# Windowed attention feeding two expert layers on one core: score products over 128 rows in place of 64, queries kept per head parity, four exp buffers in place of six

## The chip, the cores and the metric

One Trainium2 chip, one core of it. The time is device microseconds (us) of one launch. The kernel before: 823.67 us, the median of 3 runs (823.54 to 824.04).

## The reference

What is computed, in three stages. The change lies in the first.

```python
# q, k, v: (2, 8, 768, 64); n_global = 8, n_local = 96; all float32
scores = q @ k^T / 8
rel = pos[:, None] - pos[None, :]
keep = (pos[None, :] < n_global) | ((rel >= 0) & (rel < n_local))
scores = where(keep, scores - slope[h] * dist, -1e9)     # dist: |rel|, or n_local for far globals
a = exp(scores - max); a /= sum(a) + 1e-9
x = (a @ v) as (1536, 512)                               # heads side by side
xn = x / rms(x) * rms_g
x = (silu(xn @ w_gate) * (xn @ w_val)) @ w_out           # 512 -> 1536 -> 512
gates = top2(x @ w_router + softplus(x @ w_noise) * noise)   # 8 experts, softmax over two
out = sum over the two experts of gate * (relu(x @ w1[e]) @ w2[e])
```

## The kernel before

The 1536 tokens (two batches of 768) make 12 tiles of 128 rows; tiles 0 to 5 are the first batch, 6 to 11 the second. Attention works tile by tile and, within a tile, by four *pairs* of heads, so there are 48 pair steps.

**Per tile** (`prep`, line 312): the tile's queries and keys, 128 tokens by 8 heads by 64, are transposed on TensorE in four blocks of two heads (line 334). Heads 2c and 2c+1 share column block c: the even head lies in partitions 0 to 63 and the odd one in 64 to 127. ScalarE takes the transposed block out of PSUM (line 335). Tiles 0 to 5 keep float32 (`F32T = NB`, line 133); tiles 6 to 11 split each operand into a rounded part (ScalarE) and the rest (VectorE, lines 339 and 341). GpSimd copies the previous tile's and the global keys beside the tile's own (line 344).

**Per pair** (`scores`, line 358): for each of its two heads a product of queries and 256 keys (128 in the first tile of a batch). The operands are sliced to the head's 64 partitions (`sl`, line 370), so TensorE contracts 64 rows. In tiles 0 to 5 it is one float32 product, which the trace shows as two matmuls; in tiles 6 to 11 it is three products (rounded by rounded, rest by rounded, rounded by rest). VectorE then adds the bias and takes the row's minimum (line 380), ScalarE takes the exponential into a tile named `p` (line 383, six buffers), and one step later `turn` (line 388) transposes the two `p` tiles on TensorE (line 396) for the product with the values (`values`, lines 443 and 447). The four pairs are (0,2), (1,3), (4,6), (5,7) (line 115): both heads of a pair have the same parity.

**The order.** Pair steps 0 to 11 (tiles 0 to 2) run before any of the expert layer's products; there `busy` (line 213) puts three products of a blank tile behind each group, 69 in all. From step 12 on the steps are taken one by one between the products of the first layer (`up`, line 617, and `down`, line 643). The statements give the dependences; a scheduler of the framework then sets each engine's order from its own estimate of durations, and assigns the buffers of a pool in that order. Each engine works its list strictly in order. `clear_out` (line 243) writes 3 MB of zeros to the output from a small tile `zero`, which takes one of the buffers of `p`.

After the attention the rest of the first layer follows (to about 500 us), then eight expert steps of the second (lines 878, 894, 900), whose rows are gathered by indirect transfers (line 842) and transposed (line 852).

Of the kernel before, what the change touches and what calls it, by code (L numbers as in the profile page):

```python
# [9 lines left out]
F32 = mybir.dt.float32  # L10
F32R = mybir.dt.float32r
# [94 lines left out]
def fused(ctx: ExitStack, tc: tile.TileContext, q, k, v, n_global, n_local, w_gate, w_val, w_out,  # L106
# [7 lines left out]
    NP = H // 2  # L114
    pair = [(4 * (p // 2) + p % 2, 4 * (p // 2) + p % 2 + 2) for p in range(NP)]
    DC = DM // P
# [11 lines left out]
    FEED = [1, 0, 0, 0, 1, 1, 3, 2, 2, 2, 3]  # L128
    START = 12
    LAG = 8  # L130
    NRAW = {"a": 12, "b": 7}
# [24 lines left out]
    def build_bias():  # L156
        rel = sb.tile([P, 2 * P], F32, name="rel", tag="n2", bufs=N2)
        msk = sb.tile([P, 2 * P], F32, name="msk", tag="s", bufs=4)
        tmp = at.tile([P, 2 * P], F32, name="tmp", tag="p", bufs=6)
        nc.gpsimd.iota(rel, pattern=[[-1, 2 * P]], base=P, channel_multiplier=1,  # L160
# [3 lines left out]
        nc.vector.tensor_mul(msk, msk, tmp)  # L164
        rel0 = at.tile([P, P], F32, name="rel0", tag="p", bufs=6)
        msk0 = at.tile([P, P], F32, name="msk0", tag="p", bufs=6)
        nc.vector.tensor_scalar(rel0, rel[:, P:], -float(n_local), None, op0=ALU.add)
# [36 lines left out]
    def small_loads():  # L204
# [4 lines left out]
        nc.sync.dma_start(nz, noise.rearrange("(t p) e -> p t e", p=P))  # L209
    blank = sb.tile([P, 512], BF16, name="blank")  # L210
    nc.gpsimd.memset(blank, 0.0)

    def busy(k, behind):

        pz = ps.tile([P, 512], F32, name=f"idle{behind.ins.name}", tag="v")
        for _ in range(k):
            follow(nc.tensor.matmul(pz, blank[:, :P], blank, start=True, stop=True).ins, behind.ins)

# [24 lines left out]
    def clear_out():  # L243
        zero = at.tile([P, P], F32, name="zero", tag="p", bufs=6)
        nc.gpsimd.memset(zero, 0.0)
        nc.sync.dma_start(out.rearrange("(p t) (c d) -> p (t c) d", p=P, d=P),
                            zero.rearrange("p (o d) -> p o d", o=1).broadcast_to([P, NT // P * DC, P]))
# [15 lines left out]
    def follow(a, b):  # L263
        tc.add_manual_dep(a, b.name, mybir.DependencyInfo(mybir.DependencyClass.NoSync, mybir.DependencyReason.DATA),
                          reason="order")

    xTh = {}
    xTl = {}
# [37 lines left out]
    def vsplit(ti, vn):  # L306
# [3 lines left out]
        return vn, rn  # L310

    def prep(ti, wide):
        b, i = divmod(ti, NB)
# [6 lines left out]
        if full:  # L320
            kT = [at.tile([P, NP, 2 * P], F32, name=f"kT{ti}", tag="kT0", bufs=2)] * 2
            qT = [at.tile([P, NP, P], F32, name=f"qT{ti}", tag="qT0", bufs=2)] * 2
        else:
            kT = [at.tile([P, NP, 2 * P], F32R, name=f"kT{ti}_{x}", tag=f"kT{x}", bufs=2) for x in range(2)]
            qT = [at.tile([P, NP, P], F32R, name=f"qT{ti}_{x}", tag=f"qT{x}", bufs=2) for x in range(2)]
        operands = ((kn, kT[0][:, :, P:], kT[1][:, :, P:], 1.0), (qn, qT[0], qT[1], -(D ** -0.5)))
        p3s = {}
        for cs, src, dh, dl, sc in ([(slice(0, NP),) + o for o in operands] if ti else
                                    [(slice(x, x + NP // 2),) + o for x in (0, NP // 2) for o in operands]):
            if sc not in p3s:  # L330
                p3s[sc] = bank("t", wide, f"pt{ti}").rearrange("p (a b) -> p a b", a=NP)
            p3 = p3s[sc]
            for c in range(cs.start, cs.stop):
                nc.tensor.transpose(p3[:, c, :], src.rearrange("p (a t) d -> p a (t d)", a=NP)[:, c, :], ident)
            nc.scalar.activation(dh[:, cs], p3[:, cs], AF.Copy, scale=sc)
            if full:
                continue
            if sc == 1.0:
                nc.vector.tensor_sub(dl, p3, dh.bitcast(F32))
            else:  # L340
                nc.vector.scalar_tensor_tensor(dl, p3, sc, dh.bitcast(F32), op0=ALU.mult, op1=ALU.subtract)

# [15 lines left out]
    def scores(u, wide):  # L358
# [9 lines left out]
        for t in range(2):  # L368
            h = pair[pr][t]
            sl = slice((h % 2) * D, (h % 2 + 1) * D)  # L370
            o = psc[:, t * W:(t + 1) * W]
            prods = ((0, 0), (1, 0), (0, 1)) if ti >= F32T else ((0, 0),)
            for n, (a, c) in enumerate(prods):
                mm = nc.tensor.matmul(o, qT[a][sl, h // 2, :], kT[c][sl, h // 2, C0:], start=(n == 0), stop=(n == len(prods) - 1))
        if wide:
            busy(3, mm)
        for t in range(2):
            h = pair[pr][t]
            s = sb.tile([P, 2 * P], F32, name=f"s{ti}_{h}", tag="s", bufs=4)
            nc.vector.tensor_tensor_reduce(s[:, :W], nb[:, h, :], psc[:, t * W:(t + 1) * W], 1.0, BIG * 10,  # L380
                                           op0=ALU.add, op1=ALU.min, accum_out=mx[:, h:h + 1])
            p = at.tile([P, 2 * P], F32, name=f"p{ti}_{h}", tag="p", bufs=6)
            nc.scalar.activation(p[:, :W], s[:, :W], AF.Exp, scale=-1.0, bias=mx[:, h:h + 1],  # L383
# [34 lines left out]
    def values(u, wide):  # L418
# [18 lines left out]
        for t in range(2):  # L437
            h = pair[pr][t]
            hs = slice(h * D, (h + 1) * D)
# [698 lines left out]
```

## Time and profile before

| | before |
|---|---|
| median of 3 runs | 823.67 us (823.54 to 824.04) |
| the profiled execution's span | 824.3 us |
| TensorE matmuls (PE) busy | 790.2 us (96%) |
| VectorE (DVE) busy | 456.8 us (55%) |
| ScalarE (ACT) busy | 358.3 us (43%) |
| GpSimd (POOL) busy | 298.7 us (36%) |
[...]
| line 374 (score products) | 240 matmul records, 47.5 us busy |

All times in the text are us from the start of the span unless ns is written. PE is the matmul side of TensorE, PEld its weight loads, which run beside it. Matmuls are pipelined: a row's duration runs from its start to its modelled end and overlaps its neighbours', so what a matmul costs the queue is the step from its start to the next start, not its duration. In a merged row (x6) the start is the first one's, and the duration runs to the last one's end.

### The profile page before, as it was taken

The page shows a single profiled execution, that of the slowest core. Times are in us where ns is not written, and L with a number is a line of the kernel's source. Part 1 is how long each engine was busy: PE and PEld are TensorE (multiplying, and loading weights), DVE is VectorE, ACT ScalarE, POOL GpSimd, SP SyncE. Part 2 cuts the span into 40 slices and gives each one's busy share as a digit, 9 for nine tenths or more (in the row PEclk, how much of TensorE's full clock was granted, in tenths as well). Part 3 has the DMA queues.
Part 4 walks back from the last instruction along what each step waited for, and adds up shares of the span by engine and source line. Part 5 has one row for each costly group of instructions (what it writes and reads, how often), then busy time and mean ns, then how long its engine had stood idle before and what let it go on. Part 6 is the DMA issues. An engine that isn't in the chain of part 4 may idle for free. (4 is left out here: it accounts for less than half of the span.)

```text
span 824.3 us, 13771 instructions
## 1 busy us (share of the span) xinstructions
PE 790.2 (96%) x5041; PEld 697.4 (85%) x5041; DVE 456.8 (55%) x1047; ACT 358.3 (43%) x798; POOL 298.7 (36%) x344
## 2 busy tenths in 40 slices
PE   8999999999999999999997997799999999999993
PEld 5778888988898888889896986788999999999982
DVE  4588845656478888334442566443444444445551
ACT  6766556555454343122331454343343334343430
POOL 5246521222276565001421135360434343434311
PEclk9999999999999999999998999899999999999997
DMA  8555421170233240010018003983373729272010
GB/s 185 129 141 143 130 48 27 39 192 15 78 104 121 83 128 0 1 52 23 12 20 229 26 27 107 335 255 109 106 211 121 234 94 277 75 248 73 33 40 34
DMA packets 116838, 88.76 MB, mean 108 GB/s; under 512 B 49449, under 2 KB 100649, under 8 KB 116768
## 3 DMA queue, kind: packets, MB, share of 16 engines
q1 hardware_dynamic: 107920, 65.43, 28.4%
q0 software_dynamic: 7120, 19.27, 7.0%
q10 hardware_dynamic: 1728, 3.15, 1.3%
q8 instruction: 41, 0.67, 0.4%
q14 instruction: 29, 0.24, 0.1%
HBM read 75.18 MB, written 13.34 MB: 107 GB/s over the span
## 5 line engine op out<-in xcount | busy, mean ns | idle before, releaser
L878 PE MATMUL pz<-gh,sa 128*128 128x256 f32 (+7 forms) x576 | 156.6, 339 | 0.8 <-issue 0.8
L878 PEld LDWEIGHTS pz<-gh,sa 128*128 128x128 f32 x576 | 103.3, 188 | 6.3 <-issue 1.0
L878 PE MATMUL pz<-gl,sa 128*128 128x256 f32 (+7 forms) x288 | 97.2, 338 | 0.9 <-issue 0.9
L643 PE MATMUL acc<-wo,dh 128*128 128x512 f32 x288 | 89.7, 403 | 0.1
L894 PE MATMUL ac<-zh,sb 128*128 128x480 f32 (+4 forms) x320 | 86.3, 364 | 0.0
L882 ACT ACTIVATE zh<-pz 128x256 fp32r<-128x256 f32 (+7 forms) x72 | 35.0, 487 | 110.2 <-PE pz L878 107.4
L883 DVE SCALAR_TENSOR_TENSOR zl<-pz,zh 128x256 fp32r<-128x256 f32 (+7 forms) x72 | 39.8, 552 | 75.6 <-ACT zh L882 65.3
L617 PE MATMUL pz<-xTh,wg 128*128 128x256 f32 x352 | 75.4, 289 | 0.3 <-DVE u L626 0.3
L617 PE MATMUL pz<-xTh,wv 128*128 128x256 f32 x352 | 75.1, 290 | 0.0
L599 ACT ACTIVATE sa<-wab 128x512 fp32r<-128x512 f32 x72 | 45.2, 630 | 57.0 <-PE ac L894 36.3
L617 PEld LDWEIGHTS pz<-xTh,wg 128*128 128x128 f32 x352 | 58.8, 191 | 4.6 <-issue 1.0
L630 POOL TENSOR_TENSOR dl<-u,dh 128x256 fp32r<-128x256 f32 (+1 forms) x38 | 36.9, 971 | 70.9 <-ACT dh L629 53.6
L603 DVE TENSOR_TENSOR sa<-wab,sa 128x512 fp32r<-128x512 f32 x51 | 36.7, 721 | 45.5 <-ACT sa L599 38.7
L894 PEld LDWEIGHTS ac<-zh,sb 128*128 128x128 f32 x320 | 57.9, 188 | 3.1
L617 PEld LDWEIGHTS pz<-xTh,wv 128*128 128x128 f32 x352 | 59.0, 193 | 0.5
L643 PEld LDWEIGHTS acc<-wo,dh 128*128 128x128 f32 x288 | 51.3, 190 | 9.3 <-issue 0.3
L878 PEld LDWEIGHTS pz<-gl,sa 128*128 128x128 f32 x288 | 54.3, 189 | 3.8 <-issue 1.1
L383 ACT ACTIVATE p<-s,mx 128x256 f32<-128x256 f32 (+1 forms) x96 | 46.3, 484 | 24.8 <-DVE mx L380 24.5
L783 POOL DMA_INDIRECT metad<-meta,si x24 | 24.5, 1023 | 84.2 <-DVE si L762 78.1
L842 POOL DMA_INDIRECT xg<-x2d,ic x30 | 30.0, 999 | 68.9 <-PE pg L852 62.4
L643 PE MATMUL acc<-wo,dl 128*128 128x512 f32 x144 | 54.1, 403 | 0.0
L894 PE MATMUL ac<-zl,sb 128*128 128x480 f32 (+4 forms) x160 | 53.0, 357 | 0.0
(251 smaller groups left out, 1831.7 us busy)
## 6 DMA issues: line engine op xcount, KB each, us to landing
wab<-in_moe_w_dram SPq DMA_DIRECT2D x128, 256.0 KB
rg<-in_moe_w_gate_dram SPq DMA_DIRECT2D x12, 512.0 KB
rv<-in_moe_w_val_dram SPq DMA_DIRECT2D x12, 512.0 KB
ro<-in_moe_w_out_dram SPq DMA_DIRECT2D x12, 512.0 KB
vn<-in_v_dram SPq DMA_DIRECT2D x12, 256.0 KB
out_dram<-zero SPq DMA_DIRECT2D x1, 3072.0 KB
x2d<-x ACTq DMA_DIRECT2D x12, 256.0 KB
kn<-in_k_dram SPq DMA_DIRECT2D x11, 256.0 KB
```

Of the source, the lines that this page charges most:

```text
L383: nc.scalar.activation(p[:, :W], s[:, :W], AF.Exp, scale=-1.0, bias=mx[:, h:h + 1], accum_out=sm[:, h:h + 1])
L599: cp = nc.scalar.activation(wp[:, 0], src, AF.Copy)
L603: (nc.gpsimd if pool else nc.vector).tensor_sub(wp[:, 1], src, wp[:, 0].bitcast(F32))
L617: nc.tensor.matmul(pz, a[:, cs], x[:, tt:tt + nt, c, :], start=(n == 0), stop=(n == 3 * DC - 1))
L630: (nc.gpsimd if ci < len(CHUNKS) - 1 else nc.vector).tensor_sub(dl, u, dh.bitcast(F32))
L643: nc.tensor.matmul(acc[t], a[:, tt], w, start=(f == CHUNKS[ci][0] and n == 0), stop=(end and n == 2))
L783: st = nc.gpsimd.indirect_dma_start(out=metad, out_offset=bass.IndirectOffsetOnAxis(ap=si[:, t, kk:kk + 1], axis=0), in_=meta[:, G0[g] + t ...
L842: self.last = nc.gpsimd.indirect_dma_start(out=xg[:m], out_offset=None, in_=x2d[:self.rows], in_offset=bass.IndirectOffsetOnAxis(ap=self.i ...
L878: nc.tensor.matmul(pz[:, :cap], a[:, cs], x[:, c, :cap], start=(k == 0), stop=(k == 3 * DC - 1))
L882: nc.scalar.activation(dh[:, :cap], pz[:, :cap], AF.Relu)
L883: nc.vector.scalar_tensor_tensor(dl[:, :cap], pz[:, :cap], 0.0, dh[:, :cap].bitcast(F32), op0=ALU.max, op1=ALU.subtract)
L894: nc.tensor.matmul(acc[c][:, :cap], w[:, c * P:(c + 1) * P], a[:, :cap], start=(f == 0 and k == 0), stop=(f == FB2 - 1 and k == 2))
```

## The change

- From tile 3 on (`HALF = START // NP`, 3) the queries are kept in two tiles, one with the even heads' rows and zeros in partitions 64 to 127 (`q0e`, with `q1e` for the rest part), one with the odd heads' rows and zeros in partitions 0 to 63 (`q0o`, `q1o`). The score product takes all 128 partitions; the keys of the other parity meet zeros. The zero halves are written once per batch and tile by GpSimd (`qtile`): three memsets in the first batch, six multiplications by 0 in the second. Even tiles have one buffer (even heads come first in the new order), odd ones two.
- Taking the queries out of PSUM becomes two instructions of 64 partitions each, on ScalarE in tiles 3 to 11 and on VectorE in tiles 6 to 11.
- The pairs from tile 3 on are (0,2), (4,6), (1,3), (5,7).
- `p` has four buffers in place of six, for the exponentials, for three tiles of the bias set-up and for `zero`.
- `blank` has 128 columns, read four times over by the same 512-column product.

```diff
-    pair = [(4 * (p // 2) + p % 2, 4 * (p // 2) + p % 2 + 2) for p in range(NP)]
+    def pair(ti, pr):
+        a, b = (pr // 2, pr % 2) if ti < HALF else (pr % 2, pr // 2)
+        return (4 * a + b, 4 * a + b + 2)
...
+    HALF = START // NP
...
-        zero = at.tile([P, P], F32, name="zero", tag="p", bufs=6)
+        zero = at.tile([P, P], F32, name="zero", tag="p", bufs=4)
...
+    def qtile(x, m, ti):
+        key = x, m, ti // NB
+        if key not in qz:
+            one = m == "e"
+            full = ti < F32T
+            qz[key] = t = at.tile([P, NP, P], F32 if full else F32R, name=f"q{x}{m}{ti}", tag=f"q{x}{m[0]}", bufs=1 if one else 2)
+            r = slice(D, P) if one else slice(0, D)
+            if full:
+                nc.gpsimd.memset(t[r], 0.0)
+            else:
+                nc.gpsimd.tensor_scalar(t[r], ident[r].rearrange("p (o d) -> p o d", o=1).broadcast_to([D, NP, P]),
+                                        0.0, None, op0=ALU.mult)
+        return qz[key]
...
-            qT = [at.tile([P, NP, P], F32R, name=f"qT{ti}_{x}", tag=f"qT{x}", bufs=2) for x in range(2)]
-        operands = ((kn, kT[0][:, :, P:], kT[1][:, :, P:], 1.0), (qn, qT[0], qT[1], -(D ** -0.5)))
+        if ti < HALF:
+            qa = at.tile([P, NP, P], F32, name=f"qT{ti}", tag="q1o", bufs=2)
+            qT = {(0, h): qa[(h % 2) * D:(h % 2 + 1) * D, h // 2, :] for h in range(H)}
+            qd = [(slice(0, P), qa, None)]
+        else:
+            qb = [[qtile(x, m, ti) for m in ("e", f"o{ti % 2}")] for x in range(1 if full else 2)]
+            qT = {(x, h): qb[x][h % 2][:, h // 2, :] for x in range(len(qb)) for h in range(H)}
+            qd = [(slice(m * D, (m + 1) * D), qb[0][m], qb[-1][m]) for m in range(2)]
+        operands = ((kn, [(slice(0, P), kT[0][:, :, P:], kT[1][:, :, P:])], 1.0), (qn, qd, -(D ** -0.5)))
...
-            sl = slice((h % 2) * D, (h % 2 + 1) * D)
+            sl = slice((h % 2) * D, (h % 2 + 1) * D) if ti < HALF else slice(0, P)
...
-                mm = nc.tensor.matmul(o, qT[a][sl, h // 2, :], kT[c][sl, h // 2, C0:], start=(n == 0), stop=(n == len(prods) - 1))
+                mm = nc.tensor.matmul(o, qT[a, h], kT[c][sl, h // 2, C0:], start=(n == 0), stop=(n == len(prods) - 1))
...
-            p = at.tile([P, 2 * P], F32, name=f"p{ti}_{h}", tag="p", bufs=6)
+            p = at.tile([P, 2 * P], F32, name=f"p{ti}_{h}", tag="p", bufs=4)
```

The scheduler's order moves on all engines up to the end of the attention. Three places of it follow. Names carry the tile and the pair or head: `ps10_1` holds the scores of tile 10, pair 1; `p0_5` the exponential of tile 0, head 5; `pp` are transposed `p` tiles.

TensorE, tile 10, pair 1, before:

```order
L396 MATMUL pp10_0_2454<-ident_60,p10_0_2420 128x128 x2
L396 MATMUL pp10_0_2454<-ident_60,p10_2_2424 128x128 x2
L374 MATMUL ps10_1_2462<-kT10_0_2194,qT10_0_2196 128x256
L374 MATMUL ps10_1_2462<-kT10_0_2194,qT10_1_2197 128x256
L374 MATMUL ps10_1_2462<-kT10_1_2195,qT10_0_2196 128x256
L374 MATMUL ps10_1_2462<-kT10_0_2194,qT10_0_2196 128x256
L374 MATMUL ps10_1_2462<-kT10_0_2194,qT10_1_2197 128x256
L374 MATMUL ps10_1_2462<-kT10_1_2195,qT10_0_2196 128x256
L643 MATMUL acc0_6_3005<-wo0_589,dh6_0_2779 128x512
```

The same pair now:

```order
L403 MATMUL ps10_1_2480<-kT10_0_2212,q0e6_1096 128x256
L403 MATMUL ps10_1_2480<-kT10_0_2212,q1e6_1100 128x256
L425 MATMUL pp10_0_2472<-ident_60,p10_0_2438 128x128 x2
L403 MATMUL ps10_1_2480<-kT10_1_2213,q0e6_1096 128x256
L403 MATMUL ps10_1_2480<-kT10_0_2212,q0e6_1096 128x256
L403 MATMUL ps10_1_2480<-kT10_0_2212,q1e6_1100 128x256
L425 MATMUL pp10_0_2472<-ident_60,p10_2_2442 128x128 x2
L403 MATMUL ps10_1_2480<-kT10_1_2213,q0e6_1096 128x256
L362 MATMUL pt11_2497<-ident_60,kn11_2277 128x128 x4
```

The six products of a pair stay six products of 256 columns, now over all rows; the transposes of the pair before, which stood ahead of them, stand between them.

ScalarE, the exponentials of tile 0's last pairs, with what each row waits for, before:

```order
L383 ACTIVATE p0_6_276,sm0_194<-s0_6_274,mx0_193 128x128 [waits DVE_49]
L383 ACTIVATE p0_5_301,sm0_194<-s0_5_299,mx0_193 128x128 [waits DVE_49]
L335 ACTIVATE qT1_235<-pt1_242 128x512 [waits PE_49]
L383 ACTIVATE p0_7_305,sm0_194<-s0_7_303,mx0_193 128x128 [waits DVE_49]
L402 ACTIVATE pf0_1_261<-pp0_1_254 128x2x128 [waits PE_49]
```

The same place now:

```order
L412 ACTIVATE p0_6_276,sm0_194<-s0_6_274,mx0_193 128x128 [waits DVE_49]
L364 ACTIVATE qT1_235<-pt1_242 128x512 [waits PE_49]
L412 ACTIVATE p0_5_301,sm0_194<-s0_5_299,mx0_193 128x128 [waits DVE_49,PE_49]
L431 ACTIVATE pf0_1_261<-pp0_1_254 128x2x128 [waits PE_49]
L412 ACTIVATE p0_7_305,sm0_194<-s0_7_303,mx0_193 128x128 [waits DVE_49]
```

The exponential of head 5 now also waits for TensorE: its buffer is one whose transposes must have been made, two pairs back.

ScalarE around the zero transfer, before (it is the wait on a DMA queue that counts):

```order
L383 ACTIVATE p10_5_2634,sm10_2410<-s10_5_2632,mx10_2409 128x256 [waits DVE_49]
L521 ACTIVATE xTh2_2313<-px9_2590 128x512 [waits PE_49]
L383 ACTIVATE p10_7_2638,sm10_2410<-s10_7_2636,mx10_2409 128x256 [waits DMAHW2_49,DVE_49]
L409 ACTIVATE ph10_2_2622<-pp10_2_2617 128x512 [waits PE_49]
L383 ACTIVATE p11_0_2737,sm11_2727<-s11_0_2735,mx11_2726 128x256 [waits DVE_49,Activation_49]
```

Now:

```order
L438 ACTIVATE ph10_0_2477<-pp10_0_2472 128x512 [waits PE_49]
L364 ACTIVATE kT11_0_2495<-pt11_2497 128x4x128 [waits PE_49]
L412 ACTIVATE p10_4_2489,sm10_2428<-s10_4_2487,mx10_2427 128x256 [waits DVE_49,Activation_49]
L412 ACTIVATE p10_6_2493,sm10_2428<-s10_6_2491,mx10_2427 128x256 [waits DMAHW2_49,DVE_49]
L653 ACTIVATE u6_3_3134<-pz6_3_3109 128x256 [waits PE_49,Pool_49]
```

The exponential that takes over the buffer of `zero`, and so waits for the 3 MB transfer, stands in tile 10's pair 1 in place of pair 3.

## Rows read from the trace of the kernel before

**Rows 1.** Busy time in stretches: us, PE, PEld, DVE, ACT, POOL, clock, DMA, GB/s.

```profile
57.00:100.00 43.00, 43.00 (x292) 36.05 (x290) 36.16 (x91) 25.81 (x72) 24.36 (x30) 1.00 0.50 135
100.00:218.00 118.00, 118.00 (x1146) 105.14 (x1146) 68.94 (x207) 66.39 (x187) 29.81 (x47) 1.00 0.24 59
218.00:444.00 226.00, 224.43 (x1314) 194.89 (x1314) 136.10 (x281) 79.75 (x148) 90.83 (x87) 0.99 0.22 65
```

**Rows 2.** Timeline of PE around one pair's score products: start, us, instruction.

```profile
128.66 0.28 PE L617 MATMUL pz<-xTl,wg 128*128 128x256 f32 x1
128.77 0.28 PE L617 MATMUL pz<-xTh,wg 128*128 128x256 f32 x1
128.98 0.97 PE L374 MATMUL ps<-kT,qT 64*128 64x256 f32 x6
129.89 0.39 PE L617 MATMUL pz<-xTh,wg 128*128 128x256 f32 x1
130.11 0.28 PE L617 MATMUL pz<-xTl,wg 128*128 128x256 f32 x1
```

**Rows 3.** Timeline of PEld (weight loads) in the same stretch.

```profile
128.98 0.77 PEld L374 LDWEIGHTS ps<-kT,qT 64*128 64x128 f32 x6
129.89 0.19 PEld L617 LDWEIGHTS pz<-xTh,wg 128*128 128x128 f32 x1
130.00 0.19 PEld L617 LDWEIGHTS pz<-xTl,wg 128*128 128x128 f32 x1
```

**Rows 4.** Timeline of PE: first and last of the 40 groups from tile 3 on.

```profile
39.63 1.13 PE L374 MATMUL ps<-kT,qT 64*128 64x256 f32 x4
...
209.53 0.97 PE L374 MATMUL ps<-kT,qT 64*128 64x256 f32 x6
```

**Rows 5.** Timeline of PE: transposes of 64 rows, then of 128 rows, in expert steps.

```profile
574.98 0.38 PE L878 MATMUL pz<-gl,sa 128*128 128x480 f32 x1
575.20 0.37 PE L878 MATMUL pz<-gh,sa 128*128 128x480 f32 x1
575.50 0.46 PE L852 MATMUL pg<-ident,xg 64*128 64x64 f32 x4
...
736.11 0.34 PE L878 MATMUL pz<-gh,sa 128*128 128x392 f32 x1
736.29 0.60 PE L852 MATMUL pg<-ident,xg 128*128 128x128 f32 x4
```

**Rows 6.** Groups by line and shape: busy us, mean ns, idle before.

```profile
L335 ACT ACTIVATE qT<-pt 128x512 fp32r<-128x512 f32 x6 | 3.6, 598 | 4.8 <-PE pt L334 4.8
L341 DVE SCALAR_TENSOR_TENSOR qT<-pt,qT 128x512 fp32r<-128x512 f32 x6 | 4.1, 680 | 0.2 <-ACT qT L335 0.2
L558 POOL TENSOR_SCALAR wcv<-wcv 128x512 f32<-128x512 f32 x10 | 7.6, 760 | 4.8 <-ACT wcv L557 4.7
```

**Rows 7.** Timelines of POOL and PE in the start: the keys of tile 1 and their first use.

```profile
12.29 0.30 POOL L344 TENSOR_SCALAR kT<-kg 128x128 f32<-128x128 f32 x1
...
15.59 1.14 PE L374 MATMUL ps<-kT,qT 64*128 64x256 f32 x8
```

**Rows 8.** Timelines of ACT and PE: an exponential of tile 2 pair 1, two pairs' transposes.

```profile
28.99 0.49 ACT L383 ACTIVATE p<-s,mx 128x256 f32<-128x256 f32 x1
...
32.18 0.66 PE L396 MATMUL pp<-ident,p 128*128 128x128 f32 x4
...
36.96 0.60 PE L396 MATMUL pp<-ident,p 128*128 128x128 f32 x4
```

**Rows 9.** The zero transfer's issue, its stretch, and tile 10 pair 1's second exponential.

```profile
L246 SPq DMA_DIRECT2D out_dram<-zero x1: 650/650/650, 170.5 to 170.5; - x1
...
171.80:184.00 12.20, 12.20 (x116) 10.92 (x117) 6.85 (x22) 7.74 (x22) 2.93 (x6) 1.00 0.92 259
...
183.47 0.49 ACT L383 ACTIVATE p<-s,mx 128x256 f32<-128x256 f32 x1
```

**Rows 10.** A stretch in which the granted clock was low.

```profile
374.00:377.30 3.30, 3.30 (x18) 3.30 (x17) 0.00 (x0) 0.41 (x1) 0.00 (x0) 0.50 0.00 0
```

More of the change, by code (lines that the diff above doesn't have):

```diff
@@ L158, in build_bias @@
         msk = sb.tile([P, 2 * P], F32, name="msk", tag="s", bufs=4)
-        tmp = at.tile([P, 2 * P], F32, name="tmp", tag="p", bufs=6)
+        tmp = at.tile([P, 2 * P], F32, name="tmp", tag="p", bufs=4)
         nc.gpsimd.iota(rel, pattern=[[-1, 2 * P]], base=P, channel_multiplier=1,
@@ L164, in build_bias @@
         nc.vector.tensor_mul(msk, msk, tmp)
-        rel0 = at.tile([P, P], F32, name="rel0", tag="p", bufs=6)
-        msk0 = at.tile([P, P], F32, name="msk0", tag="p", bufs=6)
+        rel0 = at.tile([P, P], F32, name="rel0", tag="p", bufs=4)
+        msk0 = at.tile([P, P], F32, name="msk0", tag="p", bufs=4)
         nc.vector.tensor_scalar(rel0, rel[:, P:], -float(n_local), None, op0=ALU.add)
@@ L209, in small_loads @@
         nc.sync.dma_start(nz, noise.rearrange("(t p) e -> p t e", p=P))
-    blank = sb.tile([P, 512], BF16, name="blank")
+    blank = sb.tile([P, P], BF16, name="blank")
     nc.gpsimd.memset(blank, 0.0)
@@ L216, in busy @@
         for _ in range(k):
-            follow(nc.tensor.matmul(pz, blank[:, :P], blank, start=True, stop=True).ins, behind.ins)
+            follow(nc.tensor.matmul(pz.rearrange("p (a b) -> p a b", a=4), blank,
+                                    blank.rearrange("p (o d) -> p o d", o=1).broadcast_to([P, 4, P]), start=True, stop=True).ins, behind.ins)
     tri = sb.tile([P, P], BF16, name="tri")
@@ L321, in prep @@
             kT = [at.tile([P, NP, 2 * P], F32, name=f"kT{ti}", tag="kT0", bufs=2)] * 2
-            qT = [at.tile([P, NP, P], F32, name=f"qT{ti}", tag="qT0", bufs=2)] * 2
         else:
             kT = [at.tile([P, NP, 2 * P], F32R, name=f"kT{ti}_{x}", tag=f"kT{x}", bufs=2) for x in range(2)]
-            qT = [at.tile([P, NP, P], F32R, name=f"qT{ti}_{x}", tag=f"qT{x}", bufs=2) for x in range(2)]
-        operands = ((kn, kT[0][:, :, P:], kT[1][:, :, P:], 1.0), (qn, qT[0], qT[1], -(D ** -0.5)))
+        if ti < HALF:
[7 more added lines that the diff above has]
+        operands = ((kn, [(slice(0, P), kT[0][:, :, P:], kT[1][:, :, P:])], 1.0), (qn, qd, -(D ** -0.5)))
         p3s = {}
-        for cs, src, dh, dl, sc in ([(slice(0, NP),) + o for o in operands] if ti else
+        for cs, src, dst, sc in ([(slice(0, NP),) + o for o in operands] if ti else
                                     [(slice(x, x + NP // 2),) + o for x in (0, NP // 2) for o in operands]):
@@ L334, in prep @@
                 nc.tensor.transpose(p3[:, c, :], src.rearrange("p (a t) d -> p a (t d)", a=NP)[:, c, :], ident)
[L335 to L341, printed above, removed]
+            for rs, dh, dl in dst:
+                nc.scalar.activation(dh[rs, cs], p3[rs, cs], AF.Copy, scale=sc)
+                if full:
+                    continue
+                if sc == 1.0:
+                    nc.vector.tensor_sub(dl, p3, dh.bitcast(F32))
+                else:
+                    nc.vector.scalar_tensor_tensor(dl[rs], p3[rs], sc, dh[rs].bitcast(F32), op0=ALU.mult, op1=ALU.subtract)
         def same(dst, src):
@@ L377, in scores @@
         for t in range(2):
-            h = pair[pr][t]
+            h = pair(ti, pr)[t]
             s = sb.tile([P, 2 * P], F32, name=f"s{ti}_{h}", tag="s", bufs=4)
@@ L437, in values @@
         for t in range(2):
-            h = pair[pr][t]
+            h = pair(ti, pr)[t]
             hs = slice(h * D, (h + 1) * D)
```

3 lines of the change are left out of this document (2 added, 1 removed).

## The prediction

> **What bounds the kernel now.** I read the stretches first, then the waits of PE, then single steps of its queue. From 57 to 218 us, the part of the attention that is mixed with the first layer, PE is busy for the whole of each stretch at a granted clock of 1.00 [rows 1], and the list of waits has no row for PE there at all. VectorE comes next: 36.2 of 43.0 us from 57 to 100, then 68.9 of 118. After 218 the picture is the same (224.4 of 226 up to 444), and where the list of waits names PE at all, it is for routing and gathered rows, which follow from PE's own products and so move with them. So the kernel is as long as PE's queue, and what PE saves in the attention should move everything after it forward.
>
> A full queue may still have holes, because a busy row overlaps its neighbours. The steps show them. Around one pair of tile 8 [rows 2], a product of 256 columns with 128 rows steps 0.11 to 0.12 us (128.66 to 128.77). From the last of these to the first score product it is 0.21 (128.77 to 128.98): 0.09 too much. Six score products then take 0.91 (128.98 to 129.89) where six steps of 0.118 would take 0.71: 0.20 too much. After the change back, the first full-row product steps 0.22 (129.89 to 130.11): 0.10 too much. Within the group, only the first step (0.22 to the second start) and the last (0.21) are long, the four between are 0.118. The weight loads [rows 3] tell why: PE usually loads the next weights one product ahead (at 130.00 for the product of 130.11), but both at 128.98 and at 129.89 the load starts together with its own product. So at each change of 128 rows to 64 and back, the queue empties, and the next load is bare.
>
> **The change part by part.**
>
> *Removed: the two changes per group.* From tile 3 on there are 36 pairs; four are cut in two by other work, which makes 40 groups, from 39.63 to 209.53 [rows 4]. Taking each one's four long steps against the ordinary step of the same form, I get on average 0.094 + 0.099 + 0.090 + 0.086 = 0.369 us (the last term is small where short value products follow, 0.10 to 0.11 where a layer's products do). 40 x 0.369 = **14.8 us**. Tiles 0 to 2 keep their changes. That row count is the cause, and not something in line 374, is seen far from the attention [rows 5]: a transpose of 64 rows comes 0.30 us after a product whose step is 0.22 (574.98 to 575.20), 0.08 too much; one of 128 rows comes 0.18 after a product of 392 columns, which by 0.22 x 392/480 is just its step.
>
> *The products themselves* keep their number, columns and passes; a full-row product of 256 columns steps 0.12 [rows 2], the 64-row ones 0.118 inside the group. I cost 128 rows at 0.
>
> *Queries out of PSUM twice.* A row's time goes with the elements per partition, and these stay 512: 9 more on ScalarE at 0.60 (5.4 us), 6 more on VectorE at 0.68 (4.1 us) [rows 6]. Between 100 and 218 both are busy under 60% [rows 1], and the odd half is needed only at the third pair; 0. Uncovered, the VectorE part would cost 4.1.
>
> *Nine zero fills on POOL.* No such row exists; a 512-element row of POOL took 0.76 [rows 6], so 6.8 us at most and nothing at least. Four stand early in POOL's queue, ahead of the bias tables and of tile 1's keys. Those keys were ready at 12.6 (12.29 + 0.30) and first used at 15.59 [rows 7]: 3.0 us of room for 4 x 0.76 = 3.0, and the use itself comes later in the new order. 0.
>
> *Four buffers of exponentials.* A pair's exponentials now wait until the transposes two pairs back are done, and behind them on ScalarE stand the hidden layer's evictions, for which POOL and then PE's down products wait. In the old trace the exponentials of 41 pairs start after those transposes anyway; five start earlier, all in tiles 0 to 3, by 0.6 to 3.9 us, 8.7 together. The longest is shown: 28.99 against the end of transposes at 32.84 [rows 8]. In each of the five, the pair's own transposes came later than that wait is long (here at 36.96), so the same order would hide it; what else stands behind on ScalarE is less sure. Bounds 0 and 8.7; I take 1.0, near the lower one for that reason.
>
> *The zero tile holds one of the four.* Its transfer is issued at 170.5 and fills the queues to 184.0 [rows 9]. The waiter moves from tile 10's pair 3 to pair 1, whose second exponential ran at 183.47, so with nothing else moved it waits 0.5 us, with other pairs' work on PE meanwhile; at most 13.5, if the transfer's start fell on it. The trace lies at the low end: 0.
>
> *VectorE from 57 to 100.* Ten of the 40 groups lie there, 3.7 us. The stretch would be 39.3 us with 36.2 of VectorE in it, 92%. Bounds 0 and 3.7 given back; I take 0.7, nearer to 0 as 8% stay free.
>
> *The clock.* [...] It need not fall again at the same work, or may fall elsewhere: 0, with 1.7 either way.
>
> The sum for the profiled execution: 824.3 - 14.8 + 1.0 + 0.7 = 811.2. Its span lies 0.65 above the median of the runs, 823.67, so against that: 823.67 - 13.1 = **810.5**.
>
> [...] In [rows 3] the six loads of the score products, all of the same 64 rows, take 0.77 us from first start to last end while their products run, so they overlap; so do the full-row loads at 130.00. [...]
>
> **The rivals.**
>
> 1. *VectorE becomes the bound.* Both of its costs are paid: 3.7 given back from 57 to 100, and the 4.1 of the six added rows bare. 823.7 - 14.8 + 7.8 = 816.7. For it: 84% busy already from 57 to 100. Against: PE never waits for it now, and 58% after 100.
> 2. *The ring of four is too short* (the slower one). Place: ScalarE, at the start's five pairs and at the zero transfer. Price: 8.7 + 13.5 = 22.2 if all of it reaches PE; it decides once more than 14.8 does. 823.7 + 7.4 = 831. Against: in 41 pairs there is no wait, and in the five the transposes lie far enough behind [rows 8].
> 3. *Nothing is removed*: the long steps belong to the operands, and stay. 823.7, or up to 1 more. Against: [rows 5].
> 4. *Loads bare*: 192 matmul records of line 374 from tile 3 on, 0.19 us each [rows 3], are 36.5; less 14.8 it is +21.7, so 845. Against: loads of the same rows overlap in [rows 3]. [...]
>
> **How the numbers follow.** The forecast 0.79 (810.5; its own range 807 to 815), rival 1 0.12, rival 2 0.05, rival 3 0.03, rival 4 0.01. Runs of this kernel lie within 0.06% of each other, and about 0.2% (1.6 us) is what can be told from no change. Faster: 0.79 + 0.12 = 0.91. Same: rival 3, 0.03. Slower: 0.05 + 0.01 = 0.06. The range reaches from 823.7 - 14.8 - 2 x 1.7 (nothing given back, and two stretches like that of 374 gone) = 805.5, rounded to 806, to rival 1, 817; what is left out is below 2 in 10.
>
> **What would show it.** Right: six score products step 0.71 to 0.72 to what follows; no step of 0.21 or 0.22 at their edges; in the 64-row form line 374's successor has 48 records, all in tiles 0 to 2; PE still has no waits from 57 to the end of the attention; the stretches after it are those of before, some 13 us earlier. Wrong: bare loads at the edges, or PE rows among the waits that name VectorE (rival 1) or an exponential (rival 2), above all ahead of transposes in the first 50 us or within 14 us of the zero transfer's issue.

## The result, and the profile after

The changed kernel takes 815.65 us, the median of 4 runs (814.53 to 816.99); the kernel before, on the same chip, 823.61. The ratio is 0.9908, with a 95% interval of 0.9888 to 0.9928: 8.0 us less, where 13.1 were forecast.

The engine totals on the page of the changed kernel:

```profile
PE 778.2 (96%) x5041; PEld 696.2 (86%) x5041; DVE 459.6 (57%) x1053; ACT 362.6 (45%) x807; POOL 312.9 (38%) x353
```

PE is busy 12 us less, with as many matmuls. VectorE, ScalarE and POOL are busy longer, POOL by 14 us. The stretches (columns as in [rows 1]):

```profile
57.00:100.00 43.00, 42.29 (x310) 38.95 (x310) 38.10 (x90) 30.72 (x80) 30.68 (x34) 1.00 0.58 148
100.00:218.00 118.00, 116.73 (x1209) 108.88 (x1208) 77.02 (x224) 71.66 (x201) 36.73 (x55) 1.00 0.27 72
```

In [rows 1] PE filled both of these stretches completely. Now it does not. VectorE has 38.1 of the first 43.0 us instead of 36.2, and POOL 30.7 instead of 24.4.

First the products themselves. One pair of a tile of the second batch in the changed kernel, PE in order of time, with a product of the layer on each side (the counterpart of [rows 2]):

```profile
127.89 0.39 PE L646 MATMUL pz<-xTh,wg 128*128 128x256 f32 x2
128.12 0.28 PE L403 MATMUL ps<-kT,q0o 128*128 128x256 f32 x1
128.24 0.28 PE L403 MATMUL ps<-kT,q1o 128*128 128x256 f32 x1
128.36 0.40 PE L403 MATMUL ps<-kT,q0o 128*128 128x256 f32 x2
128.60 0.28 PE L403 MATMUL ps<-kT,q1o 128*128 128x256 f32 x1
128.72 0.28 PE L403 MATMUL ps<-kT,q0o 128*128 128x256 f32 x1
128.84 0.28 PE L646 MATMUL pz<-xTl,wg 128*128 128x256 f32 x1
128.96 0.60 PE L362 MATMUL pt<-ident,qn 128*128 128x128 f32 x4
```

Six steps from 128.12 to 128.84 are 0.72 us (before: 0.91), and every step is 0.11 to 0.12, the first after the group (128.84 to 128.96) too. The *drains*, as the long steps at a change of row count are called from here on, are gone. The weight loads run one product ahead, 0.19 us each, beside the products:

```profile
128.01 0.19 PEld L403 LDWEIGHTS ps<-kT,q0o 128*128 128x128 f32 x1
128.12 0.19 PEld L403 LDWEIGHTS ps<-kT,q1o 128*128 128x128 f32 x1
```

How much of that arrives? The first product of the layer's next part (pg) follows when all 12 tiles are through the attention and the first part. Before, and after:

```profile
242.06 0.39 PE L617 MATMUL pg<-xTh,wg 128*128 128x512 f32 x1
```

```profile
233.93 0.40 PE L646 MATMUL pg<-xTh,wg 128*128 128x512 f32 x1
```

The start of pg comes 8.1 us earlier. (The spans of the two profiled executions differ by 11.4 us. In its other runs the kernel before has spans some 1.8 us below their times, 822.1 for 823.94, so its profiled span of 824.3 was about 2 us longer than usual, and what goes beyond 8.1 arises behind pg.) Where the rest went stands in the list of waits of PE up to 240 us; columns: who waits for whom, us in total, times, longest:

```profile
PE pt L362 <- POOL q0e L328: 3.3, 1, 3.3
PE pz L646 <- ACT xTh L550: 1.0, 1, 1.0
PE acc L672 <- ACT dh L658: 0.8, 1, 0.8
PE pp L425 <- DVE ss L529: 0.4, 1, 0.4
PE po L476 <- ACT ph L438: 0.3, 1, 0.3
...
```

Four more rows of 0.2 follow. Before, this list had only the two rows of the launch. It counts from a product's modelled end; counted in steps, start to start against the ordinary step, the new waits are longer: 1.3 us between 58 and 86, 0.8 between 154 and 187, 2.8 between 214 and 220, 4.9 together, against 0.25 before. The last of them, the end of the attention, on PE:

```profile
214.62 0.39 PE L672 MATMUL acc<-wo,dl 128*128 128x512 f32 x1
215.77 1.20 PE L672 MATMUL acc<-wo,dh 128*128 128x512 f32 x4 [0.76 <-ACT dh L658]
217.14 0.74 PE L672 MATMUL acc<-wo,dl 128*128 128x512 f32 x2 [0.17 <-POOL dl L659]
217.71 0.63 PE L545 MATMUL px<-ident,x 128*128 128x128 f32 x4
219.30 0.50 PE L646 MATMUL pz<-xTh,wg 128*128 128x256 f32 x2 [0.96 <-ACT xTh L550]
220.03 0.39 PE L646 MATMUL pz<-xTl,wg 128*128 128x256 f32 x1 [0.23 <-DVE xTl L551]
```

Steps of 1.15, 1.6 and 0.7 us: PE has nothing left to put between a product and the evictions that its successor needs. Before, a whole block of 24 products of the layer stood behind the last values (222.00 to 224.75) and covered these. In the new scheduled order 13 of the 24 stand ahead of them. Throughout, the attention now stands further behind the layer: 77 of the layer's products are ahead of the end of tile 3 instead of 58, and 577 instead of 546 at the end of tile 11.

The books up to pg: 8.1 arrived, 4.6 went into waits, and 0.7 into the start (the same product of the blank tile at 14.46 instead of 13.76). Together that is 13.4 of the 14.8 us; for the other 1.4 I found no single place. Seven steps of 0.31 instead of 0.12 between 46 and 91 us look like a loss and are none:

```profile
78.04 1.02 PE L403 MATMUL ps<-kT,q0o 128*128 128x256 f32 x4
78.71 0.59 PE L646 MATMUL pz<-xTh,wg 128*128 128x256 f32 x2
79.14 0.28 PE L646 MATMUL pz<-xTl,wg 128*128 128x256 f32 x1
```

In these float32 tiles a score product steps 0.216 us, with 64 rows as with 128. Four of them and two of the layer's at 0.118 should take 1.10, and from 78.04 to 79.14 it is 1.10: the last of the four is recorded with a step of only 0.03, and the step behind it is longer by as much.

### The profile page after: what moved, and what is told of

Read it like the earlier page. It is cut to its first block, busy times and chain, and to the rows that moved or that the text cites. A ratio compares the mean times of both kernels' runs of the same rounds, so it can differ in the third digit from the quotient of the medians.

```text
span 812.9 us, 13827 instructions
## 1 busy us (share of the span) xinstructions
PE 778.2 (96%) x5041; PEld 696.2 (86%) x5041; DVE 459.6 (57%) x1053; ACT 362.6 (45%) x807; POOL 312.9 (38%) x353
## 5 line engine op out<-in xcount | busy, mean ns | idle before, releaser
L911 ACT ACTIVATE zh<-pz 128x256 fp32r<-128x256 f32 (+7 forms) x72 | 35.1, 487 | 110.0 <-PE pz L907 110.0
L646 PE MATMUL pz<-xTh,wg 128*128 128x256 f32 x352 | 73.7, 288 | 1.2 <-ACT xTh L550 1.0
L632 DVE TENSOR_TENSOR sb<-wab,sb 128x512 fp32r<-128x512 f32 x67 | 47.1, 703 | 8.9 <-ACT sb L628 8.0
```

The costliest lines, as they stand in the source:

```text
L632: (nc.gpsimd if pool else nc.vector).tensor_sub(wp[:, 1], src, wp[:, 0].bitcast(F32))
L646: nc.tensor.matmul(pz, a[:, cs], x[:, tt:tt + nt, c, :], start=(n == 0), stop=(n == 3 * DC - 1))
L911: nc.scalar.activation(dh[:, :cap], pz[:, :cap], AF.Relu)
```

## The experiments

**Theory** at this point: the drains cost what was forecast, and the change's other parts (the ring of four exponential buffers, the zero fills, the second evictions of the queries) put holes into PE's queue. **Rivals**: the gain comes from the new order, or the drains were worth less.

Of all runs, the median, that of the kernel before in the same session, and two readings of the profile: the start of pg, and PE's longest wait for gathered rows near 500 us, which will matter.

| run | median | before | difference | pg at | wait for rows |
|---|---|---|---|---|---|
| the change | 815.65 | 823.61 | -8.0 | 233.93 | 5.0 |
| rows64 | 829.98 | 823.94 | +6.0 | 247.55 | 6.1 |
| ring4 | 830.07 | 823.94 | +6.1 | 245.44 | 8.5 |
| fills_act | 815.31 | 823.94 | -8.6 | 230.98 | 9.5 |
| half0 | 816.73 | 823.94 | -7.2 | 236.44 | 5.9 |
| n2_3 | 815.13 | 822.49 | -7.4 | 233.46 | 4.5 |
| ring5 | 813.67 | 822.49 | -8.8 | 234.79 | 6.5 |
| tail_hold | 815.94 | 822.49 | -6.6 | 233.09 | 6.9 |
| late_words | 812.96 | 822.62 | -9.7 | 233.64 | 5.9 |
| before_late_words | 826.44 | 822.62 | +3.8 | 246.72 | 6.5 |
| no_low_words | 815.19 | 822.62 | -7.4 | 233.54 | 6.9 |
| all_four | 816.97 | 824.05 | -7.1 | 230.62 | 9.2 |
| fills_dve | 814.90 | 824.05 | -9.2 | 230.52 | 8.6 |

The granted clock differs from run to run of one kernel: half0 took 813.5 us at a mean of 0.987 and 820.65 at 0.979. In the profiled runs it falls to 0.50 for some stretches. In the one of [rows 10] twelve of the layer's products of 256 columns, from 374.43 to 376.99, step 0.213 us each, against 0.11 to 0.12 at 1.00 [rows 2]. PE's busy time in the stretches at 0.50, up to 700 us, is 13.7 us in the kernel before, 13.4 in the changed one, 6.8 in ring5 and 23.1 in half0. An estimate: if, as those steps suggest, about half of that time is lost, this alone is 3 to 12 us in a run. So a difference of 1 to 3 us between two medians need not come from the edit.

### The row count alone

```diff
-            sl = slice((h % 2) * D, (h % 2 + 1) * D) if ti < HALF else slice(0, P)
+            sl = slice((h % 2) * D, (h % 2 + 1) * D)
...
-                mm = nc.tensor.matmul(o, qT[a, h], kT[c][sl, h // 2, C0:], start=(n == 0), stop=(n == len(prods) - 1))
+                mm = nc.tensor.matmul(o, qT[a, h] if ti < HALF else qT[a, h][sl], kT[c][sl, h // 2, C0:], start=(n == 0), stop=(n == len(prods) - 1))
```

> The changed kernel in its own order on every engine, with its queries, zeros and four exp buffers, but the score products of tiles 3 to 11 contract only the 64 rows of their head. In this order they stand in 48 groups. Theory (the row count empties PE's queue at each change): 48 x 0.369 = 17.7 us come back in steps of 0.21 to 0.22 at the edges, less what falls into the 4.9 us in which PE of the changed kernel waits for ScalarE, VectorE and POOL: 13 to 18 us more than the changed kernel's 815.65, so 829 to 833. Rival (the gain came from the new pair order or from the scheduler's other order): within 2 us of 815.65, and no long steps.

829.98 us (828.58 to 831.72), ratio to the kernel before 1.0068 (1.0054 to 1.0083): 14.3 us more than the changed kernel, in the same order on every engine. PE, one pair in the same surroundings as above:

```profile
133.72 0.39 PE L646 MATMUL pz<-xTh,wg 128*128 128x256 f32 x2
134.04 0.38 PE L403 MATMUL ps<-kT,q0o 64*128 64x256 f32 x1
134.26 0.28 PE L403 MATMUL ps<-kT,q1o 64*128 64x256 f32 x1
134.38 0.40 PE L403 MATMUL ps<-kT,q0o 64*128 64x256 f32 x2
134.62 0.28 PE L403 MATMUL ps<-kT,q1o 64*128 64x256 f32 x1
134.73 0.28 PE L403 MATMUL ps<-kT,q0o 64*128 64x256 f32 x1
134.94 0.39 PE L646 MATMUL pz<-xTl,wg 128*128 128x256 f32 x1
135.17 0.38 PE L362 MATMUL pt<-ident,qn 128*128 128x128 f32 x2
```

The four long steps are back (0.20 in, 0.22, 0.21, and 0.23 after), 0.90 for six products, with everything else unchanged. So the row count is the cause. The size fits too: the long steps of the 48 groups come to some 16 us (less than 48 x 0.369, as many pieces are short), and PE's other waits from 15 to 240 us shrink from 4.9 to 3.4 us in steps, which leaves 14.5. The same run shows the other side: with the drains back, the change costs 6.0 us against the kernel before, of which eight more groups (48 instead of 40) are 2 to 3 us.

### The ring of four alone

```diff
-            p = at.tile([P, 2 * P], F32, name=f"p{ti}_{h}", tag="p", bufs=6)
+            p = at.tile([P, 2 * P], F32, name=f"p{ti}_{h}", tag="p", bufs=4)
```

(and the four other tiles of that tag, in the kernel before)

> The kernel before with four exp buffers instead of six, nothing else. Theory (forecast 1.0, bounds 0 to 8.7): within 1.5 us of the kernel before, no PE wait that names an exponential. Rival (the ring took the part of the 14.8 us that did not arrive): 4 to 7 us slower than the kernel before, with PE waits ahead of transposes in the first 60 us.

830.07 us (826.75 to 831.6), ratio 1.0064 (1.0045 to 1.0082): 6.1 us slower. The size is the rival's, but the mechanism is neither's: no wait of PE names an exponential. Its trace shows three other things. The scheduler, with fewer buffers, cuts the 36 pairs into 46 groups instead of 40, six more drains of 0.37, 2.2 us. At the end of the attention PE waits 1.45 us in steps instead of 0.25. And the wait for gathered rows is longer; from 500 to 525 us, ring4 and the kernel before:

```profile
PE pg L852 <- DMA xg<-x2d,ic: 9.7, 2, 8.5
```

```profile
PE pg L852 <- DMA xg<-x2d,ic: 6.9, 2, 5.6
```

2.8 us there. The three are 6.2 us, near the 6.1 measured, but the account does not close: the two profiled spans differ by only 5.3, and the third wait is longer because 16 products that stood ahead of it now stand behind it. What the profile shows firmly is pg 3.4 us later, which is the first two. The first costs nothing with 128 rows, where every step is 0.11 to 0.12; the other two are costs of the order.

### POOL's fills, and 128 rows from the start

Two single changes of the changed kernel. In fills_act the six fills of rounded tiles move to ScalarE:

```diff
-                nc.gpsimd.tensor_scalar(t[r], ident[r].rearrange("p (o d) -> p o d", o=1).broadcast_to([D, NP, P]),
-                                        0.0, None, op0=ALU.mult)
+                nc.scalar.activation(t[r], ident[r].rearrange("p (o d) -> p o d", o=1).broadcast_to([D, NP, P]), AF.Copy, scale=0.0)
```

> The changed kernel with the six fp32r zero fills on ScalarE instead of POOL (1.5 to 1.8 us each there). Theory (POOL's fills push the attention back behind the layer's products in the scheduled order: 77 products of the first layer stand ahead of the end of tile 3 instead of 58, 577 instead of 546 at the end of tile 11, so that a block of 24 products no longer follows the last values): here 59 and 564 stand there, the block of 24 is back, PE's waits between 210 and 222 us fall from 2.8 to under 0.6 and all its waits from 4.9 to under 3; 2 to 4 us less than the changed kernel, 811.5 to 813.5. Rival (the waits come from the queries' second evictions on ScalarE and VectorE): six more ScalarE instructions of 0.6 us make it the same or up to 2 us slower, and the waits stay.

What the fills cost on POOL in the changed kernel (min, median and max in ns, first and last start):

```profile
L330 POOL TENSOR_SCALAR q1o<-ident x2: 1486/1490/1493, 27.2 to 36.2; 64x512 fp32r<-64x512 f32 x2
...
L330 POOL TENSOR_SCALAR q0o<-ident x2: 1497/1711/1925, 79.2 to 101.7; 64x512 fp32r<-64x512 f32 x2
L330 POOL TENSOR_SCALAR q1e<-ident x1: 1522/1522/1522, 4.8 to 4.8; 64x512 fp32r<-64x512 f32 x1
L330 POOL TENSOR_SCALAR q0e<-ident x1: 1814/1814/1814, 87.9 to 87.9; 64x512 fp32r<-64x512 f32 x1
```

That is twice the bound that the prediction had, or more. Without them pg starts 2.95 us earlier, the waits at the end halve (1.45 us; under 0.6 were expected) and those from 57 to 100 shrink to one of 0.64. But the time is 815.31 (814.03 to 816.48), the same, where 811.5 to 813.5 was expected: near 500 us PE waits 9.5 us for gathered rows instead of 5.0. Most of what the attention gained is given back there.

In half0 the new pairs and 128 rows hold from the first tile on:

```diff
-    HALF = START // NP
+    HALF = 0
```

> The changed kernel with 128 rows from the first tile on (the pairs of tiles 0 to 2 in the new order too). Theory: nine groups fewer change the row count, 9 x 0.37 = 3.3 us at most; but where two neighbouring pairs of opposite parity ran beside each other in tiles 0 to 2, that is lost (eight records took 0.72 us there, one after another they take 0.90 at full clock), some 0.2 us for each of up to five such places, and three more zero fills stand in POOL's queue. In the scheduled order the block of 24 products again follows the last values, so PE's waits between 210 and 222 us fall under 0.6: 811 to 814. Rival (what the opposite parity gave is worth more than the changes of row count, or the start is bound elsewhere): 816 or more.

816.73 (813.5 to 820.65), with pg at 236.44 in the profiled run (819.74), 2.5 us later than in the changed kernel. In the start PE now waits for VectorE. Stretches of half0 around it:

```profile
21.00:24.00 3.00, 0.87 (x4) 0.47 (x3) 2.97 (x9) 1.38 (x5) 2.89 (x4) 0.95 0.59 178
24.00:27.00 3.00, 3.00 (x10) 2.14 (x10) 1.67 (x8) 2.55 (x10) 1.50 (x2) 0.50 0.57 178
27.00:33.00 6.00, 6.00 (x42) 4.99 (x41) 1.33 (x7) 4.42 (x13) 0.78 (x2) 0.99 0.34 77
```

PE works 0.87 of 3.00 us, VectorE and POOL nearly all of it, and in the 3 us behind this hole the granted clock is 0.50. The median is the rival's (816 or more), but it does not decide: three of the six runs lie at 813.5 to 815.1, and in the profiled one the two stretches at 0.50 before pg cost some 3.4 us (half of 6.8), by the same estimate, which is more than the 2.5 by which pg is late.

### Is it the ring, or VectorE?

Six buffers were not tried beside the doubled queries; a fifth takes the room of one of the four buffers of the normalised rows. So n2_3 is the control with that alone, and ring5 has the fifth buffer too:

```diff
-    N2 = 4
+    N2 = 3
...
-            p = at.tile([P, 2 * P], F32, name=f"p{ti}_{h}", tag="p", bufs=4)
+            p = at.tile([P, 2 * P], F32, name=f"p{ti}_{h}", tag="p", bufs=5)
```

> The control for the run after it: the changed kernel with three instead of four buffers for the normalised rows, which frees 2 KB. The order of the attention is that of the changed kernel on every engine; only gathered rows of the last stage are fetched later. All theories: PE waits of 2.8 us between 210 and 222 us as in the changed kernel; the time within 2 us of 815.65, with any difference after 600 us.

> The control with five exp buffers instead of four. Theory (the ring of four makes the attention late in the scheduled order, so that the first layer's products are used up before its end and PE waits): the order is back to 53 products of the layer ahead of the end of tile 3 and 538 at the end of tile 11 (the kernel before has 58 and 546, the changed kernel 77 and 577), a block of 24 follows the last values, PE's waits up to 222 us fall from 4.9 to under 1.5 us: 3 to 5 us less than the control, about 811 to 812.5 if the control is at 815.65. Rival (POOL's zero fills or the second evictions of the queries make the waits, whatever the ring): within 1.5 us of the control, and the waits stay.

The control is the changed kernel (815.13, 814.46 to 818.73; the same waits). ring5: 813.67 (812.84 to 815.78), 1.5 us less where 3 to 5 were expected, with intervals of the ratios that overlap (0.9883 to 0.9918, and 0.9899 to 0.9938). Half of the theory fell. The order is back as expected, and the wait at the end of the attention is 0.24 us. But pg starts 1.3 us later than in the control, because the waits only changed their place. The better time goes with the clock. The sums over the stretches at 0.50 up to 700 us, for the control (365.4 to 368.8, 437.1 to 443.9, 495.1 to 498.5, 508.8 to 512.2) and for ring5 (439.1 to 442.5, 504.0 to 510.8):

```profile
sum 17.00, PE 13.55 PEld 12.81 DVE 2.60 ACT 3.58 POOL 1.65; mean PE 3.39 PEld 3.20 DVE 0.65 ACT 0.89 POOL 0.41
sum 10.20, PE 6.83 PEld 6.06 DVE 1.80 ACT 1.58 POOL 1.55; mean PE 3.42 PEld 3.03 DVE 0.90 ACT 0.79 POOL 0.78
```

PE's sums differ by 6.7 us; half of that is more than the 2.0 us between these two runs (815.33 and 813.3). From 57 to 100 us, the stretch, then the waits of PE:

```profile
57.00:100.00 43.00, 39.80 (x288) 36.16 (x286) 40.31 (x91) 29.93 (x78) 28.02 (x33) 1.00 0.56 142
```

```profile
PE po L472 <- DVE vn L445: 2.0, 2, 1.2
PE pz L646 <- DVE u L655: 1.1, 1, 1.1
```

VectorE is busy 40.3 of 43.0 us, and PE waits for it, 4 us in steps. This is the first cost of rival 1 of the prediction, which it had at 3.7. With four buffers the scheduler fills that stretch with products of the layer instead, and lacks them at the end. A third run holds them back by order alone:

```diff
+                if f == 3 and t0 == 8 and nm == "g" and n == 0:
+                    follow(mm.ins, state["last"].ins)
```

(`state["last"]` is the last product of the values; four buffers)

> The changed kernel with one more order: the last block of 24 products of the first layer's part that runs beside the attention may not start before the last values of tile 11. Four buffers stay. Theory (the end of the attention costs 2.8 us of waits because that block is used up too early): the waits between 210 and 222 us fall to under 1.2 us, of which up to 1 us comes back ahead of the last values, where 13 of the block's products covered an eviction: 1 to 2 us less than the changed kernel, 813.5 to 814.7. Rival (the waits only move ahead of the last values): within 0.7 us of 815.65.

815.94 (812.53 to 817.32), pg at 233.09: the wait at the end falls from 2.8 to 1.4 us, the others grow by 0.4, 0.8 us arrive at pg and are lost behind it: 6.9 us of wait for gathered rows instead of 5.0. In time it can't be told from no change.

### VectorE's load

no_low_words is ring5 without the third VectorE instruction of each conversion of weights:

```diff
-        nc.vector.scalar_tensor_tensor(wi, lo, 29, wi, op0=ALU.logical_shift_right, op1=ALU.bitwise_or)
```

> The kernel with five exp buffers, and the third VectorE instruction of every conversion left out (the three low bits of each first-layer weight that come from its second word are missing, so the output differs in the last bits): some ten VectorE instructions of 0.7 to 1.1 us fewer from 57 to 100 us. Theory (VectorE is the bound there): VectorE under 36 of 43 us, PE's waits there under 1.5 us instead of 4.5, 2.5 to 4.5 us less than 813.67: 809 to 811. Rival (latencies of chains or POOL): the waits stay above 3 us, within 1 us.

The stretch of 57 to 100 us in it:

```profile
57.00:100.00 43.00, 43.00 (x316) 39.81 (x315) 35.06 (x87) 31.77 (x84) 30.31 (x36) 1.00 0.58 158
```

VectorE has 35.1, and PE waits for nothing there. That speaks for its load as the bound; it does not prove it, as the scheduler's order moved too (316 matmuls in the stretch, 288 in ring5). The time that was expected of it did not come (815.19, 813.62 to 816.82): with VectorE out of the way the scheduler used up the block at the end again (2.7 us of waits from 214 to 220), and pg is at 233.54.

late_words leaves nothing out. Two conversions whose weights are not needed before 220 us are emitted later and ordered behind tile 7:

```diff
-            feed(FEED[vi] if vi < len(FEED) else 0)
+            feed((FEED[vi] if vi < len(FEED) else 0) - (vi == 0 and f == 3) + (vi == 4 and f == 0))
...
+        if marks and f == 4 and nm != "o":
+            follow(ab.ins, marks[-1])
```

> The kernel with five exp buffers, and two conversions of weights that are only needed after 220 us (the gate and value words of the fifth block, three VectorE instructions each, 0.7 us each when undisturbed and up to 2.3 beside POOL) held back from 57 to 100 us until after tile 7. Theory (with the drains gone VectorE is the bound from 57 to 100 us, 40.3 of 43.0 us busy, and PE waits 4.5 us for it there): those waits fall by at least half, to under 2.2 us, the end of the attention stays covered: 2 to 4 us less than with five buffers alone, 809.5 to 811.5 against its 813.67. Rival (the waits are latencies of single chains, not VectorE's load): within 1 us of it, the waits stay.

> The kernel before (six exp buffers, 64 rows) with the same two conversions held back. Theory (there PE's queue with its drains is longer than VectorE's work from 57 to 100 us, so VectorE's relief is worth nothing): within 1 us of the kernel before, up to 1 us slower as the end of the attention has one transposed tile less ahead of it in the scheduled order. Rival (VectorE already held the kernel before): 2 us or more faster.

812.96 (811.32 to 817.89), the least median, but 0.7 below ring5 and not apart from it. VectorE has 39.2 of the 43.0 us there (40.3 in ring5): only one of some four microseconds left, as what moved up took the place, and the waits stay at 3.4 us. Expected were under 2.2. In the kernel before, the same edit was expected to do nothing and cost 3.8 us (824.75 to 828.06): no wait from 57 to 100 us appears or goes, but its order has 47 groups instead of 40, seven more drains, 2.6 us at 0.37 each, and 1.0 us more of waits at the end. So there VectorE did not hold PE, and in that kernel both changed orders (ring4 and this one) were paid in drains.

The last two put several of these together: all_four has five buffers, the fills on ScalarE, the late conversions and the held block; fills_dve has five buffers, late conversions, and the fills on VectorE. In fills_dve the late conversions are also emitted one place earlier than in late_words (`vi == 3` for `vi == 4`). Its fills:

```diff
-                nc.gpsimd.tensor_scalar(t[r], ident[r].rearrange("p (o d) -> p o d", o=1).broadcast_to([D, NP, P]),
+                nc.vector.tensor_scalar(t[r], ident[r].rearrange("p (o d) -> p o d", o=1).broadcast_to([D, NP, P]),
```

> What the runs point to, together: 128 rows as in the change, five exp buffers, the six fp32r fills on ScalarE, the two late conversions held back, and the last block of 24 products kept for after the last values. Theory (what the drains left behind is VectorE's work from 57 to 100 us, lengthened where it stands beside POOL's, and the uncovered end): PE's waits after 15 us and up to 222 fall from 4.9 in the changed kernel to under 2.5 us; 2.5 to 4 us less than its 815.65, 811 to 813, and the least of all runs if the clock falls no oftener. Rival (each relief moves the wait to the next place): waits still over 4 us, 814 or more.

> Five exp buffers and the two late conversions held back, as before, but the six fp32r fills on VectorE. They are then more work for VectorE (six of 0.4 to 0.7 us, three or four of them from 57 to 100 us) and less for POOL, whose fills of 1.5 to 1.9 us lengthen VectorE's neighbours. Theory (what VectorE loses beside POOL is more than a fill costs it): VectorE's busy time from 57 to 100 us not above the 39.2 with the fills on POOL, PE's waits there not above 3.4 us, time within 1.5 us of 812.96 or less. Rival (VectorE's own instructions are what counts): 1 to 2 us more of PE's waits there.

Both bring pg to 230.6 and 230.5, 11.5 us ahead of the kernel before, with PE's waits from 15 to 222 us at 2.6 and 1.8 us in steps: the attention then gives most of what the drains were worth. But the times are 816.97 (814.17 to 818.1), where 811 to 813 was expected, and 814.90 (813.73 to 816.31), 1.9 above late_words where at most 1.5 was, though VectorE's busy time (37.7) and PE's waits came as expected. The wait near 500 us in all_four:

```profile
506.69 1.09 PE L884 MATMUL pg<-ident,xg 128*128 128x128 f32 x4 [9.21 <-DMA xg<-x2d,ic]
```

The gathered rows come at 506.7 (changed kernel: 508.9, though its pg is 3.3 us later). In the changed kernel 16 further products of the second layer stand ahead of that wait (the last starts at 503.6), in all_four they stand behind it. That is again the scheduler's order. Why the rows come no earlier than 2.2 us for 3.3 I did not settle, and no run holds that order fixed. No run beats the changed kernel beyond its interval.

## Why the prediction was right or wrong

The time, 815.65, lies in the stated range (806 to 817) but outside the forecast's own (807 to 815): 8.0 us came of 13.1. The terms one by one:

- *The drains, 14.8 us.* Right in cause, by rows64. In size right as far as can be told: rows64's 14.3 is for 48 groups less the waits that shrank, and the books place 13.4. That PE's queue empties at the change was my reading; the rows show the long steps, and loads that start together with their own product [rows 3].
- *128-row products at the price of 64-row ones, loads beside them.* Right: steps of 0.12, in the float32 tiles 0.216 with either row count, and loads of 0.19 us beside them. Rivals 3 and 4 are out. That loads would lie bare under 128 rows no run shows: in the changed kernel they start one product ahead (at 128.01 for the product of 128.12).
- *The ring, 1.0 (bounds 0 to 8.7).* The path was wrong. I looked for exponentials that would wait in the old order; none does. But the number of buffers is an input of the scheduler, and through the order it moved the layer's products ahead of the attention. Alone the ring costs 6.1 us in the kernel before, of which 2.2 are drains that 128 rows do not pay. In the changed kernel its place is the 2.8 us of waits at the end of the attention, which a fifth buffer takes to 0.24.
- *VectorE from 57 to 100, 0.7 (bounds 0 to 3.7).* Too small: part of PE's freed time is lost with four buffers and with five, either as waits for VectorE (4 us in ring5) or as blocks used up early and missed at the end (2.8 us). I read the two as one shortage, of other work to put between a product and what it waits for; no run separates them fully. The forecast gave 1.7 us for this term and the ring together, and 4.6 went into waits. The time is nearer to rival 1 (816.7) than to the forecast, but rival 1 also counted 4.1 us of bare VectorE rows, which no run shows, so that this nearness is luck.
- *Fills, 0 (at most 6.8).* The bound was wrong: 1.5 to 1.9 us each instead of 0.76, 9.7 for six and 1.7 for three memsets of 0.52 to 0.59. Moving the six to ScalarE brings pg 2.95 us forward (fills_act), though the order changes with it.
- *The zero transfer, 0.* Right: issued at 168.9, no wait of PE or ScalarE names it.
- *Queries evicted twice, 0.* Not tried alone. The rows of 64 partitions took 0.59 us on ScalarE and 0.67 to 0.70 on VectorE, those of 128 partitions with the same 512 elements in each 0.60 and 0.68 before, as assumed.
- *What follows the attention moves with it.* Right for the change (8.1 at pg, 8.0 in the medians), not for runs whose pg came 11 us earlier.
- *The clock, 0.* Right for the pair of profiled runs: mean granted 0.985 after and 0.984 before, and PE busy 13.4 and 13.7 us at 0.50. The 1.7 either way was an estimate, half of the 3.3 us of [rows 10]; by the steps there, 0.213 us in place of 0.117, it is 1.5.
- *What can be told from no change, 1.6 us.* Too small. It rested on three runs that lie within 0.06%; over the later sessions the kernel before took 819.67 to 826.35 us.

## What to carry to other kernels

Keep neighbouring products on one row count: here a group of six 64-row products among 128-row ones cost 0.37 us more than its products on average, and by that price the six more groups of ring4 cost 2.2 us, an estimate. When a full engine is relieved, look at once for the next busiest engine of each stretch, here VectorE at 84% from 57 to 100 us, since part of the gain can end there: in ring5 PE waited for it some 4 us. Before two medians are compared, compare their clocks. And under a scheduler that sets the order, a pool's size or a moved instruction is an edit of the whole order: compare the orders, not only the waits.

## What the runs showed of the hardware

Some of VectorE's instructions take longer beside POOL's. In ring5, both engines near 56 us:

```profile
55.23 0.69 DVE L596 SCALAR_TENSOR_TENSOR wco<-ro,wco 128x512 int32<-128x512 int32 x1
55.60 1.45 POOL L600 TENSOR_TENSOR wv<-wcv,wv 128x512 fp32r<-128x512 f32 x1 [4.24 <-ACT wv L599]
55.96 1.65 DVE L597 SCALAR_TENSOR_TENSOR wco<-ro,wco 128x512 int32<-128x512 int32 x1
57.53 0.68 DVE L484 TENSOR_TENSOR x<-po,rs 128x512 f32<-128x512 f32 x1
```

The same form takes 0.69 us where it starts 0.37 ahead of POOL's instruction, and 1.65 where it starts 0.36 after it, ending 0.56 after POOL's end; PE's longest wait of the attention in that run, 1.22 us at 58.59, follows it. Against the median duration of each form, such lengthening adds some 4.5 us to VectorE from 57 to 100 in the kernel before, 7 in the changed one and 8 in ring5, nearly all of it beside a POOL instruction. Which POOL instructions lengthen which of VectorE's, and why, was not settled. Beside the fill of 87.89 to 89.70 in the changed kernel, VectorE's instructions at 88.27 and 88.95 took 0.41 and 0.68, as elsewhere; beside the fill at 79.16, the instruction at 79.31 took 0.74, where the same form took 0.42 at 92.34 (line 589). So some 7 of VectorE's 38.1 busy us in that stretch of the changed kernel are lengthening, little of it beside the fills. With the fills on VectorE itself (fills_dve) VectorE was busy 37.7 of 43.0 us, less than the 39.2 of late_words with them on POOL, but the two runs differ in the order as well.
